# Moving the log-decay sums behind the first chunk's scores in a scan and feed-forward kernel

## The chip, the cores and the metric

The kernel runs on one core of one Trainium2 chip. The metric is the device time of one execution in microseconds (us). Five engines work side by side, each through its own list of instructions in order: TensorE (PE in the rows, its weight loads PEld), VectorE (DVE), ScalarE (ACT), GpSimd (POOL) and SyncE (SP), whose queue issues all DMA transfers here.

## The reference

```python
log_a = np.log(np.clip(a, 1e-06, 1.0))
for c in range(nc):
    cum = np.cumsum(la, axis=-1)                      # la, xc, Bc, Cc: chunk c
    L = np.exp(cum[:, :, :, None] - cum[:, :, None, :]) * causal
    CB = np.einsum('bhin,bhjn->bhij', Cc, Bc)
    y_intra = np.einsum('bhij,bhjd->bhid', CB * L, xc)
    y_inter = np.einsum('bhin,bhnd->bhid', Cc, state) * np.exp(cum)[:, :, :, None]
    y[:, :, sl] = y_intra + y_inter
    decay_from_j = np.exp(cum[:, :, -1:] - cum)
    Bx = np.einsum('bhjn,bhjd->bhjnd', Bc, xc) * decay_from_j[:, :, :, None, None]
    state = decay_full[:, :, None, None] * state + np.sum(Bx, axis=2)
x = y.transpose(0, 2, 1, 3).reshape(B * S, H * D)     # 3072 tokens, 256 wide
h = x @ w_in                                          # to 2048
out = np.maximum(0.01 * h, h) @ w_out                 # back to 256
```

## The kernel before

The program walks the sequence in 16 chunks of 48 positions, with all 32 pairs of batch and head in one chunk. A chunk has a fixed series of steps: `scores` (TensorE, C times B, into a PSUM tile `sc`), a decay exponential `decay_exp` (ScalarE, from a PSUM tile `pd` into `lt`), `weigh` (VectorE, scores times decays), `state_decay` (GpSimd, writes the state rows of `lt` from `erev`), `chunk_products` (TensorE, `lt` times `xs`), a transpose into `stage` and copies of the new state into the next chunk's `xs` (`hand_on`). The next chunk's products need these copies, so the chunks form a serial chain. The feed-forward part runs on 512-token tiles beside the later chunks: `ffn_in` (six matmuls into `hp`), an activation into `gh`, a rest `gl`, and `ffn_out`. Weights come as words `raw`, are decoded (`decode_abs` on ScalarE into `mag`, then VectorE) and split into a high part `wh` (ScalarE) and a low part `wl` (GpSimd).

The order of the instructions on every engine is the order in which the Python code is written. Waits between engines are put in by the framework from the tiles that instructions read and write.

The decays come in two ways. Chunks 0 to 2 take `decay_mask` and `decay_direct`, which multiply by `reach` (made on VectorE from the log decays `la`). Chunks 3 to 15 take `decay_stack`, which reads `dl` and `dr`. Part of these are rows of 16-bit pieces of running sums: `sums` (L222) multiplies `la` by `ends_at` into the PSUM tile `first`, `split_sums` (L228) makes three 16-bit parts in four passes (L232 ScalarE, L233 VectorE, L235 ScalarE, L237 VectorE), `save_sums` (L239) stores them to DRAM in two DMAs, and `load_rows` (L248) loads the rows of one chunk in two DMAs, `dl` (L253) and `dr` (L256). `fill_rest` (L208) fills another part of `dr` on ScalarE. `reverse_near` (L600) writes other columns of the same PSUM tile `first` with four small matmuls, and ScalarE's exponential of them (L610) gives `erev`, from which GpSimd makes the state rows (L321).

`keep_warm` (L117) issues matmuls on a zeroed tile `idle` whose result nobody reads; four of them open the program, two more stand at the second feed-forward step (`BRIDGE`).

Of the kernel before, what the change touches and what calls it, by code (L numbers as in the profile page):

```python
# [19 lines left out]
Q = 48  # L20
# [9 lines left out]
TS = 512  # L30
LAG = 3
OUT_AT = {1: 0, 2: 1, 3: 2, 4: 3, 5: 4, 8: 5}
WARM = 4
BRIDGE = {1: 2}
RAWS = 3
SLOTS = 2
# [25 lines left out]
def scan_ffn(ctx: ExitStack, tc: tile.TileContext, a_l, c_l, d_l, x_l, w_l, out_l):  # L62
# [46 lines left out]
    def fetch_x(c, eng=nc.sync):  # L109
        alloc_x(c)  # L110
        for rows in [slice(h * R + N, h * R + R) for h in range(2)] if c > 1 else [slice(0, 2 * R)]:
            eng.dma_start(xss[c][rows].rearrange("p h b d -> p (h b d)"), x_l[c, rows])
# [1 line left out]
    idle = const.tile([128, 944], BF16, name="idle")  # L114
    nc.vector.memset(idle[:, :128], 0.0)

    def keep_warm(space, n):  # L117
        for _ in range(n):
            nc.tensor.matmul(
                space, lhsT=idle[:, :128],  # L120
                rhs=idle[:, :128].unsqueeze(1).to_broadcast([128, TS // 128, 128]),
                start=True, stop=True,
            )

    nc.scalar.preload_act_table_set("natural_log_exp_and_others")
    first = banks()
    keep_warm(first[:, 1], WARM)

    la = pe.tile([128, NC * NM], F32, name="la")
    nc.sync.dma_start(la, a_l)  # L130
# [77 lines left out]
    def fill_rest(b):  # L208
        nc.scalar.copy(
            dr[:Q, b].rearrange("q m i -> q (m i)").bitcast(F32).rearrange(  # L210
                "q (m i) -> q m i", m=NM
            ),
            later[:Q].bitcast(F32).unsqueeze(1).to_broadcast([Q, NM, Q // 2]),
        )
# [7 lines left out]
    def sums(space):  # L222
        for hf in range(2):
            nc.tensor.matmul(
                space[:, hf, :2 * Q], lhsT=la[:R + Q, hf * 128:(hf + 1) * 128],
                rhs=ends_at[:R + Q].rearrange("p g i -> p (g i)"), start=True, stop=True,
            )

    def split_sums(space):
        total = space[:, :, :2 * Q].rearrange("p f (g i) -> p f g i", i=Q)  # L230
        p = [parts[:, :, :, i] for i in range(3)]
        nc.scalar.copy(p[0], total)  # L232
        nc.vector.tensor_tensor(out=rest, in0=total, in1=p[0], op=ALU.subtract)  # L233
        yield
        nc.scalar.copy(p[1], rest)  # L235
        yield
        nc.vector.tensor_tensor(out=p[2], in0=rest, in1=p[1], op=ALU.subtract)  # L237

    def save_sums(f, eng=nc.sync):  # L239
        eng.dma_start(  # L240
            left_d[:, f * 8:(f + 1) * 8].rearrange("g c m t i -> (c m) g (t i)"),
            parts[:, f].rearrange("p g t i -> p g (t i)"),
        )
        eng.dma_start(
            right_d[f * 8:(f + 1) * 8].rearrange("c m q i -> (c m) (q i)"),
            parts[:, f].rearrange("p g t i -> p (g t i)"),
        )
# [20 lines left out]
    def decay_direct(c, space):  # L268
        for k in range(2):
            for g in range(2):  # L270
                h, rows = half(g, 2 * k), slice(g * R, g * R + Q)
                nc.tensor.matmul(
                    space[h * R:(h + 1) * R, k, :8 * Q], lhsT=after[rows, g],
                    rhs=reach[c][rows, 8 * k:8 * k + 8], start=False, stop=True,
                )
# [29 lines left out]

    spread = {}

    def spread_c(c):
        if c >= SPREAD:
            spread[c] = ins[c][:, C_AT:].rearrange("p (b e i) -> p b e i", b=NB, e=2)  # L310
            return
        cs = spread[c] = pcs.tile([128, NB, 2, Q], F32, name="cs")
        src = ins[c][:, C_AT:NEAR].rearrange("p (b i) -> p b i", b=NB)
        for e in range(2):
            nc.scalar.activation(cs[:, :, e], src, AF.Copy, scale=mine[:, e:e + 1])

    def state_decay(c):
        if c + 1 == NC:
            return
        alloc_lt(c)  # L320
        nc.gpsimd.tensor_tensor(  # L321
            out=lts[c].rearrange("q p b e r -> q (p b e) r")[:, :, :N],
            in0=ins[c][:, N_AT:N_AT + NM * N].rearrange("p (m n) -> p m n", n=N),
            in1=erev[:, c * NM:(c + 1) * NM].unsqueeze(2).to_broadcast([128, NM, N]),
            op=ALU.mult,
        )
# [187 lines left out]
    def ffn_in(s, warm=0):  # L514
        t, f = steps[s]
        assert f in ready
        hp = hps[s] = ps_h.tile([128, TS], F32, name="hp")
        keep_warm(hp, warm)
        n = 0
        for h, x in ((0, xh), (0, xl), (1, xh)):  # L520
            for k in range(2):
                nc.tensor.matmul(  # L522
                    hp, lhsT=w_half[h][:, f, k * 128:(k + 1) * 128], rhs=x[t][:, k, :],
                    start=(n == 0), stop=(n == 5),
                )
                n += 1
        ghs[s] = pg.tile([128, TS], F32R, name="gh")
        gls[s] = pg.tile([128, TS], F32R, name="gl")
        nc.scalar.activation(ghs[s], hp, AF.Prelu, alpha=0.01)  # L529
# [45 lines left out]
    with tc.tile_pool(name="ps_d", bufs=2, space=PSUM, reuse_waits="tile") as ps_d:  # L575

        def free_tile():
            return ps_d.tile([128, 2, TS], F32, name="pd")
# [23 lines left out]
        def reverse_near(space, at):  # L602
            for k in range(2):
                for g in range(2):
                    h, rows = half(g, 2 * k), slice(g * R, g * R + Q)
                    nc.tensor.matmul(
                        space[h * R:(h + 1) * R, k, at:at + near // 2], lhsT=after[rows, g],
                        rhs=by_pair(la[:, :near], rows, k), start=True, stop=True,
                    )
            nc.scalar.activation(  # L610
                erev[:, :near].rearrange("q (c k m) -> q k c m", k=2, m=4),
                space[:, :, at:at + near // 2].rearrange("q k (c m) -> q k c m", m=4), AF.Exp,
            )
# [18 lines left out]
            decay_mask(pd)  # L632
        fill_reach(0, 0)
        fill_reach(0, 1)
        sums(first)
        decay_direct(0, pds[0])
        nc.vector.tensor_reduce(out=mine, in_=own, axis=mybir.AxisListType.X, op=ALU.add)
        fill_reach(2, 0)
        splitting = split_sums(first)
        next(splitting)  # L640
        spread_c(0)
        fill_reach(1, 0)
        next(splitting)
        for _ in splitting:
            pass
        fill_reach(1, 1)
        save_sums(0)
        sc = banks()
        scores(0, sc)
        decay_exp(0, pds[0])  # L650
        reverse_near(first, 2 * Q)
        decay_direct(1, pds[1])
        state_decay(0)
        weigh(0, sc)
        spread_c(1)
        decay_exp(1, pds[1])
        fill_rest(3 % SLOTS)
        state_decay(1)
        os = free_tile()
        chunk_products(0, os)  # L660
        fetch_x(2)
        fetch_w(1)
        load_rows(3)
        load_rows(4)
        fetch_c(3)
        scs = {1: banks()}
        scores(1, scs[1])
# [8 lines left out]
        lows(0, os)  # L676
        spread_c(2)
        decay_exp(2, pd)
        fill_rest(4 % SLOTS)
        state_decay(2)  # L680
        decode_shift(0)
        decode_sign(0)
# [5 lines left out]
        for h in range(2):  # L688
            reverse(pd[:, h], rest_of[h], 8 * Q)
        fetch_w(2)  # L690
        fetch_c(4)
        fetch_x(3)
        states(1, os, (1, 2, 0, 2, 1, 2, 0, 0))
# [9 lines left out]
        settle()  # L703
        highs(2, os)
        decode_abs(1)
        lows(2, os)
        turn(2, os)
        decode_shift(1)
# [385 lines left out]
```

## Time and profile before

| | |
|---|---|
| median of 3 runs | 303.44 us (303.3 to 304.85) |
| the profiled execution's own time | 303.38 us |
| its span, first to last instruction | 301.5 us |
| around the span | 1.88 us |
| TensorE busy | 293.6 us (97% of the span) |
| VectorE, ScalarE, GpSimd busy | 218.3, 182.4, 71.9 us |

The profile page is of one execution. Busy shares are averages over stages with different limits; the stages are told apart in the rows further down.

### The profile page before, as it was taken

What the parts mean: (1) busy time and instruction counts of PE and PEld (TensorE: products, weight loads), DVE (VectorE), ACT (ScalarE), POOL (GpSimd) and SP (SyncE); (2) the same over time, 40 slices, a digit from 0 to 9 for tenths busy, and PEclk for the clock granted to TensorE, in tenths of its full rate; (3) what the DMA queues carried; (4) which work ended last, traced back from release to release, by engine and by line L of the source; (5) the groups of instructions that cost most, each with busy time, mean ns of one, the idle gap of its engine ahead of it and who ended that gap; (6) DMA issues with size and microseconds to landing.
All of it is one profiled execution on the core that took longest, in us unless ns stands there. A gap on an engine that the chain in (4) does not pass through costs nothing.

```text
span 301.5 us, 6819 instructions
## 1 busy us (share of the span) xinstructions
PE 293.6 (97%) x2718; PEld 230.9 (77%) x2718; DVE 218.3 (72%) x379; ACT 182.4 (61%) x351; POOL 71.9 (24%) x148
## 2 busy tenths in 40 slices
PE   8889999999999999999999999999999999999995
PEld 4547676777777778888888888888888888888883
DVE  6879979987875688866877887677576565656562
ACT  6989758666755565735555666574665364536452
POOL 7567666866865440000000000000000000000000
PEclk9999999999999999999999999999999999999999
DMA  6697658665532101000100000000030000000004
GB/s 235 213 315 245 199 173 252 206 222 174 161 93 93 28 5 67 0 2 0 70 2 1 0 0 3 0 0 0 2 139 0 0 2 1 0 0 2 0 0 139
DMA packets 12492, 22.95 MB, mean 76 GB/s; under 512 B 4590, under 2 KB 5486, under 8 KB 12462
## 3 DMA queue, kind: packets, MB, share of 16 engines
q1 hardware_dynamic: 12462, 22.53, 23.2%
q8 instruction: 21, 0.34, 0.5%
q14 instruction: 9, 0.07, 0.1%
HBM read 19.08 MB, written 3.44 MB: 75 GB/s over the span
## 4 chain that ended last, share of the span: by engine, by line
PE 89%; DVE 5%; ACT 2%; issue 1%; DMA 1%; POOL 0%; SPq 0%; DVEq 0%
PE sc L776 18%; PE op L806 14%; PE sc L806 14%; PE op L546 14%; PE hp L522 13%; PE hp L776 7%; PE sc L366 3%; PE sc L336 2%; PE sc L280 1%; DVE mag L463 1%; DVE top L468 1%; DMA dr<-right_d 1%; DVE w L477 1%; DVE gl L535 1%; DVE lt L350 1%
## 5 line engine op out<-in xcount | busy, mean ns | idle before, releaser
L412 POOL COPY xs<-stage 16x128 f32<-16x128 f32 x98 | 35.8, 365 | 24.5 <-DVE stage L396 18.2
L529 ACT ACTIVATE gh<-hp 128x512 fp32r<-128x512 f32 x32 | 19.1, 598 | 26.0 <-PE hp L522 25.8
L817 ACT ACTIVATE gh<-u 128x512 fp32r<-128x512 f32 x32 | 20.0, 625 | 17.7 <-DVE u L858 17.7
L546 PE MATMUL op<-gh,wh 128*128 128x512 f32 x64 | 27.9, 436 | 0.0
L821 DVE TENSOR_TENSOR gl<-u,gh 128x512 fp32r<-128x512 f32 x32 | 22.0, 687 | 7.9 <-ACT u L818 7.9
L857 DVE TENSOR_TENSOR u<-sc,kept 128x512 f32<-128x512 f32 x16 | 11.1, 691 | 22.2 <-PE sc L776 22.2
L817 ACT ACTIVATE gh<-kept 128x512 fp32r<-128x512 f32 x16 | 10.1, 633 | 28.1 <-DVE kept L866 28.1
L817 ACT ACTIVATE gh<-hp 128x512 fp32r<-128x512 f32 x16 | 9.6, 598 | 26.8 <-PE hp L776 26.8
L546 PE MATMUL op<-gl,wh 128*128 128x512 f32 x64 | 25.2, 394 | 0.4 <-DVE gl L535 0.4
L866 DVE TENSOR_TENSOR kept<-sc,kept 128x512 f32<-128x512 f32 x16 | 11.1, 692 | 19.4 <-PE sc L776 19.3
L546 PE MATMUL op<-gh,wl 128*128 128x512 f32 x64 | 25.0, 390 | 0.0
L806 PE MATMUL op<-gl,wh 128*128 128x512 f32 x64 | 24.9, 389 | 0.0
L806 PE MATMUL sc<-gl,wh 128*128 128x512 f32 x64 | 24.9, 389 | 0.0
L806 PE MATMUL sc<-gh,wl 128*128 128x512 f32 x64 | 24.9, 389 | 0.0
L806 PE MATMUL op<-gh,wh 128*128 128x512 f32 x64 | 24.9, 389 | 0.0
L806 PE MATMUL op<-gh,wl 128*128 128x512 f32 x64 | 24.9, 389 | 0.0
L806 PE MATMUL sc<-gh,wh 128*128 128x512 f32 x64 | 24.9, 389 | 0.0
L350 DVE TENSOR_TENSOR lt<-sc,lt 128x384 f32<-128x384 f32 x32 | 16.3, 550 | 10.7 <-ACT gh L529 8.1
L535 DVE TENSOR_TENSOR gl<-hp,gh 128x512 fp32r<-128x512 f32 x32 | 21.7, 677 | 3.1 <-ACT hp L532 3.1
L491 POOL TENSOR_TENSOR wl<-w,wh 128x512 fp32r<-128x512 f32 x16 | 20.7, 1301 | 9.6 <-ACT wh L490 9.4
L522 PE MATMUL hp<-xh,wh 128*128 128x512 f32 x64 | 20.3, 398 | 0.8 <-ACT xh L423 0.6
L818 ACT ACTIVATE u<-u 128x512 f32<-128x512 f32 x32 | 20.2, 632 | 1.0
(147 smaller groups left out, 733.1 us busy)
## 6 DMA issues: line engine op xcount, KB each, us to landing
raw<-w_l SPq DMA_DIRECT2D x16, 512.0 KB, 4.1
bcn<-d_l SPq DMA_DIRECT2D x13, 448.0 KB, 5.1
xs<-x_l SPq DMA_DIRECT2D x28, 96.0 KB, 3.4
out_l<-ob SPq DMA_DIRECT2D x10, 256.0 KB, 2.0
bcn<-c_l SPq DMA_DIRECT2D x3, 352.0 KB
xs<-x_l SPq DMA_DIRECT2D x2, 256.0 KB, 5.1
out_l<-ob SPq DMA_DIRECT2D x4, 128.0 KB
dl<-left_d SPq DMA_DIRECT2D x13, 9.0 KB, 3.7
```

The source lines that it names most:

```text
L350: nc.vector.tensor_tensor(out=to, in0=at, in1=to, op=ALU.mult)
L412: copy(xss[c + 1][h * R:h * R + N, 2 * p:2 * p + 2, bs], stage[rows, :, bs],)
L491: nc.gpsimd.tensor_tensor(out=wl[:, f], in0=w32s[f], in1=wh[:, f], op=ALU.subtract)
L522: nc.tensor.matmul(hp, lhsT=w_half[h][:, f, k * 128:(k + 1) * 128], rhs=x[t][:, k, :], start=(n == 0), stop=(n == 5),)
L529: nc.scalar.activation(ghs[s], hp, AF.Prelu, alpha=0.01)
L535: nc.vector.tensor_tensor(out=gls[s], in0=hps.pop(s), in1=ghs[s], op=ALU.subtract)
L546: nc.tensor.matmul(op, lhsT=w_half[h][:, f, DM + m * 128:DM + (m + 1) * 128], rhs=x, start=(start and i == 0), stop=(last and i == 2),)
L776: nc.tensor.matmul(bank, lhsT=w[h], rhs=x[g], start=start and i == 0, stop=i == 2, skip_group_check=True,)
L806: nc.tensor.matmul(outs[t][m], lhsT=w_half[h][:, f, DM + m * 128:DM + (m + 1) * 128], rhs=x, start=start and i == 0, stop=last and i == 2,)
L817: nc.scalar.activation(gh, h, AF.Prelu, alpha=0.01)
L818: nc.scalar.activation(in_place, h, AF.Prelu, alpha=0.01)
L821: nc.vector.tensor_tensor(out=gl, in0=g, in1=gh, op=ALU.subtract)
```

## The change

- The two `sums` matmuls leave their place ahead of the first `decay_direct`; two dummy matmuls of 512 and 384 columns (`BETWEEN`) stand there. The sums now come behind `reverse_near`.
- `split_sums` moves behind `weigh(0)`, its passes between the two halves of `spread_c(1)`; its last pass goes from VectorE to GpSimd.
- `save_sums(0)` comes behind `fetch_x(2)`, and `load_rows(3)` and `load_rows(4)` move behind `fetch_w(2)`.
- `fill_rest` for chunk 3 takes the place of that for chunk 4, which moves behind `decode_abs(1)`.

```diff
+BETWEEN = (4, 3)
-    def keep_warm(space, n):
-        for _ in range(n):
+    def keep_warm(space, lengths):
+        for n in lengths:
             nc.tensor.matmul(
-                space, lhsT=idle[:, :128],
-                rhs=idle[:, :128].unsqueeze(1).to_broadcast([128, TS // 128, 128]),
+                space[:, :n * 128], lhsT=idle[:, :128],
+                rhs=idle[:, :128].unsqueeze(1).to_broadcast([128, n, 128]),
                 start=True, stop=True,
             )
...
-        nc.vector.tensor_tensor(out=p[2], in0=rest, in1=p[1], op=ALU.subtract)
+        nc.gpsimd.tensor_tensor(out=p[2], in0=rest, in1=p[1], op=ALU.subtract)
...
-        sums(first)
+        keep_warm(first[:, 1], BETWEEN)
         decay_direct(0, pds[0])
         nc.vector.tensor_reduce(out=mine, in_=own, axis=mybir.AxisListType.X, op=ALU.add)
         fill_reach(2, 0)
-        splitting = split_sums(first)
-        next(splitting)
         spread_c(0)
         fill_reach(1, 0)
-        next(splitting)
-        for _ in splitting:
-            pass
         fill_reach(1, 1)
-        save_sums(0)
         sc = banks()
         scores(0, sc)
         decay_exp(0, pds[0])
         reverse_near(first, 2 * Q)
+        sums(first)
         decay_direct(1, pds[1])
         state_decay(0)
         weigh(0, sc)
-        spread_c(1)
+        spread_c(1, (0,))
+        splitting = split_sums(first)
+        next(splitting)
+        spread_c(1, (1,))
+        next(splitting)
         decay_exp(1, pds[1])
-        fill_rest(3 % SLOTS)
         state_decay(1)
+        for _ in splitting:
+            pass
         os = free_tile()
         chunk_products(0, os)
         fetch_x(2)
+        save_sums(0)
         fetch_w(1)
-        load_rows(3)
-        load_rows(4)
         fetch_c(3)
...
-        fill_rest(4 % SLOTS)
+        fill_rest(3 % SLOTS)
...
         fetch_w(2)
+        load_rows(3)
+        load_rows(4)
         fetch_c(4)
...
         decode_abs(1)
+        fill_rest(4 % SLOTS)
         lows(2, os)
```

TensorE's list from the first decay matmuls to the first chunk's products, before (in brackets the semaphores that a row waits for; the words `DVE`, `Activation`, `Pool` and `DMAHW` in their names say whose work it is):

```order
L224 MATMUL sc<-ends_at,la 128x96 [waits DMAHW0_49,Activation_49,Pool_49]
...
L272 MATMUL pd<-reach_134,after 64x384 [waits DVE_49,Pool_49]
...
L336 MATMUL sc<-cs,bcn 64x96 [waits DMAHW1_49,Activation_49]
...
L606 MATMUL sc<-la,after 64x24 [waits DVE_49]
...
L272 MATMUL pd<-reach_135,after 64x384 [waits DVE_49]
...
L366 MATMUL pd<-lt,xs 32x64 [waits DMAHW2_49,DVE_49,Pool_49]
```

The sums (L224) are the first of these, and the rows left out repeat the ones shown. The same stretch of the changed kernel, its lines numbered by the new file:

```order
L120 MATMUL sc<-idle 128x512
...
L120 MATMUL sc<-idle 128x384
L273 MATMUL pd<-reach_134,after 64x384 [waits DVE_49,Pool_49]
...
L339 MATMUL sc<-cs,bcn 64x96 [waits DMAHW1_49,Activation_49]
...
L609 MATMUL sc<-la,after 64x24 [waits DMAHW0_49]
...
L225 MATMUL sc<-ends_at,la 128x96 [waits Activation_49]
...
L273 MATMUL pd<-reach_135,after 64x384 [waits DVE_49]
...
L369 MATMUL pd<-lt,xs 32x64 [waits DMAHW2_49,DVE_49,Pool_49]
```

The dummies wait for nothing; the sums stand between the small matmuls of `reverse_near` and the second `decay_direct`, and now wait for ScalarE alone. (Tile `sc` is also the name under which `first` is printed, since `banks` makes both.)

ScalarE's list over the same stretch, before:

```order
L232 CAST parts<-sc 128x4x48 [waits PE_49]
L315 ACTIVATE cs<-bcn,mine 128x4x48 [waits DMAHW1_49,DVE_49]
...
L235 CAST parts<-rest 128x4x48 [waits DVE_49]
L299 ACTIVATE lt<-pd 128x2x4x48 [waits PE_49]
...
L610 ACTIVATE erev<-sc 128x2x6x4 [waits PE_49]
L315 ACTIVATE cs<-bcn,mine 128x4x48 [waits DMAHW3_49]
...
L209 COPY dr<-later 48x384 [waits Activation_49]
L412 COPY xs<-stage 16x2x64 [waits DMAHW4_49,DVE_49]
```

One cast stands ahead of the first pair `cs`, one behind it, and the copy into `dr` ahead of the state copies. The changed kernel:

```order
L318 ACTIVATE cs<-bcn,mine 128x4x48 [waits DMAHW1_49,DVE_49]
...
L300 ACTIVATE lt<-pd 128x2x4x48 [waits PE_49]
...
L613 ACTIVATE erev<-sc 128x2x6x4 [waits PE_49]
L318 ACTIVATE cs<-bcn,mine 128x4x48 [waits DMAHW3_49]
L233 CAST parts<-sc 128x4x48 [waits PE_49]
L318 ACTIVATE cs<-bcn,mine 128x4x48
L236 CAST parts<-rest 128x4x48 [waits DVE_49]
...
L415 COPY xs<-stage 16x2x64 [waits DMAHW4_49,DVE_49]
```

The two casts of the sums moved to between and behind the second pair `cs`, and the copy into `dr` is gone from here. (Between the last two rows stand the two exponentials of chunk 1, as before.)

SyncE's list of DMAs from the first stores to the fourth chunk's input, before:

```order
L240 DMA left_d<-parts 128x2x144 [waits DVE_49]
L244 DMA right_d<-parts 128x288 [waits DMAHW0_49]
L112 DMA xs<-x_l 48x512 [waits DMAHW2_49,DMAHW1_49,PE_49]
...
L94 DMA raw<-w_l 128x2048 [waits DMAHW3_49]
L253 DMA dl<-left_d 48x2x48 [waits DMAHW7_49,DMAHW4_49]
L256 DMA dr<-right_d 6x16x48 [waits DMAHW5_49,DMAHW0_49]
...
L103 DMA bcn<-d_l 128x896 [waits Pool_49]
```

The stores come first, and one large transfer (`raw`) stands between them and the row loads. The changed kernel:

```order
L113 DMA xs<-x_l 48x512 [waits DMAHW2_49,PE_49]
...
L241 DMA left_d<-parts 128x2x144 [waits DMAHW1_49,Pool_49]
L245 DMA right_d<-parts 128x288
L95 DMA raw<-w_l 128x2048 [waits DMAHW3_49]
L104 DMA bcn<-d_l 128x896 [waits DMAHW4_49]
L95 DMA raw<-w_l 128x2048 [waits DMAHW5_49]
L254 DMA dl<-left_d 48x2x48 [waits DMAHW6_49,DMAHW1_49]
L257 DMA dr<-right_d 6x16x48 [waits DMAHW7_49,DMAHW2_49]
```

The stores went behind the load of chunk 2's `xs`, and between them and the first row loads there are now three large transfers where one stood. The row loads wait for their stores as before (`DMAHW1` and `DMAHW2` are the stores' semaphores here).

## Rows read from the trace of the kernel before

**Rows 1.** Stretches: us; busy of PE, PEld, DVE, ACT, POOL; clock, DMA share, GB/s.

```profile
0.00:24.00 24.00, 20.55 (x460) 11.80 (x464) 18.84 (x51) 19.69 (x51) 14.51 (x35) 1.00 0.79 255
...
60.00:140.00 80.00, 80.00 (x1019) 62.61 (x1007) 60.14 (x108) 48.23 (x94) 31.54 (x69) 1.00 0.26 80
```

**Rows 2.** Chain that ended last, 7 to 10 us: start us, us, what.

```profile
7.15 0.29 PE sc L606 x8
...
7.46 0.22 ACT erev L610
...
7.75 0.63 POOL lt L321
...
8.43 0.87 PE pd L366 x53
...
9.33 0.46 DVE stage L396
```

**Rows 3.** TensorE's timeline, 2.7 to 8 us: start us, us, instruction, count.

```profile
2.73 1.49 PE L262 MATMUL pd<-later,bars 112*128 112x384 bf16 x4
4.01 1.04 PE L224 MATMUL sc<-ends_at,la 112*128 112x96 f32 x4
4.99 1.35 PE L272 MATMUL pd<-reach,after 48*64 48x384 f32 x8
6.26 0.89 PE L336 MATMUL sc<-cs,bcn 32*64 32x96 f32 x32
...
7.22 0.91 PE L272 MATMUL pd<-reach,after 48*64 48x384 f32 x8
```

**Rows 4.** TensorE's timeline, 13 to 14 us.

```profile
13.38 0.71 PE L616 MATMUL pd<-la,after 112*128 112x80 f32 x4
```

**Rows 5.** ScalarE's timeline, 5 to 10 us; brackets: idle before it and releaser.

```profile
5.31 0.80 ACT L315 ACTIVATE cs<-bcn,mine 128x192 f32<-128x192 f32 x2
6.01 0.34 ACT L235 CAST parts<-rest 128x192 bf16<-128x192 f32 x1
...
8.26 0.86 ACT L299 ACTIVATE lt<-pd 128x384 f32<-128x384 f32 x2
9.00 0.51 ACT L209 COPY dr<-later 48x384 f32<-48x384 f32 x1
9.81 0.94 ACT L412 COPY xs<-stage 16x128 f32<-16x128 f32 x3 [0.30 <-DVE stage L396]
```

**Rows 6.** VectorE's timeline, the sums' second pass.

```profile
5.45 0.36 DVE L233 TENSOR_TENSOR rest<-sc,parts 128x192 f32<-128x192 f32 x1 [0.18 <-ACT parts L232]
```

**Rows 7.** GpSimd's timeline, 7 to 11 us.

```profile
7.75 1.52 POOL L321 TENSOR_TENSOR lt<-bcn,erev 128x256 f32<-128x256 f32 x2 [0.89 <-ACT erev L610]
9.90 0.94 POOL L412 COPY xs<-stage 16x128 f32<-16x128 f32 x3 [0.62 <-POOL lt L321]
```

**Rows 8.** ScalarE's timeline, 16 to 19 us.

```profile
17.63 1.22 ACT L412 COPY xs<-stage 16x128 f32<-16x128 f32 x4 [0.53 <-DVE stage L396]
```

**Rows 9.** SyncE's queue, 6 to 12 us: start us, us of issuing.

```profile
6.77 0.39 SPq L240 DMA_DIRECT2D left_d<-parts  x1
...
9.32 1.47 SPq L112 DMA_DIRECT2D xs<-x_l  x2
```

**Rows 10.** Time from issue to landing of the row loads (tile dl), then of tile xs.

```profile
DMA to landing us min/median/max: 2.6/3.7/4.2
DMA to landing us min/median/max: 2.1/3.8/5.1
```

**Rows 11.** TensorE's timeline, 18 to 22 us.

```profile
18.15 0.50 PE L280 MATMUL sc<-dr,dl 102*128 102x384 bf16 x2
...
20.17 0.73 PE L522 MATMUL hp<-xh,wh 128*128 128x512 f32 x2 [0.16 <-ACT wh L490]
...
21.62 0.73 PE L522 MATMUL hp<-xh,wl 128*128 128x512 f32 x2 [0.25 <-DMA dr<-right_d]
```

**Rows 12.** GpSimd's timeline, 20 to 22 us.

```profile
20.26 1.30 POOL L491 TENSOR_TENSOR wl<-w,wh 128x512 fp32r<-128x512 f32 x1 [0.48 <-ACT wh L490]
```

More of the change, by code (lines that the diff above doesn't have):

```diff
@@ L126, in scan_ffn @@
     first = banks()
-    keep_warm(first[:, 1], WARM)
+    keep_warm(first[:, 1], (TS // 128,) * WARM)
     la = pe.tile([128, NC * NM], F32, name="la")
@@ L306, in scan_ffn, with spread_c @@
     spread = {}
-    def spread_c(c):
+    def spread_c(c, es=(0, 1)):
         if c >= SPREAD:
@@ L311, in spread_c @@
             return
-        cs = spread[c] = pcs.tile([128, NB, 2, Q], F32, name="cs")
+        if c not in spread:
+            spread[c] = pcs.tile([128, NB, 2, Q], F32, name="cs")
+        cs = spread[c]
         src = ins[c][:, C_AT:NEAR].rearrange("p (b i) -> p b i", b=NB)
-        for e in range(2):
+        for e in es:
             nc.scalar.activation(cs[:, :, e], src, AF.Copy, scale=mine[:, e:e + 1])
@@ L517, in ffn_in @@
         hp = hps[s] = ps_h.tile([128, TS], F32, name="hp")
-        keep_warm(hp, warm)
+        keep_warm(hp, (TS // 128,) * warm)
         n = 0
```

## The prediction

> **What bounds the kernel now.** I read the stretches of the span first, since the change touches only the opening. From 60 to 140 us TensorE is busy all the time; in the first 24 us it is busy for 20.55 [rows 1]. The reader is to see that all of the change lies in those 24 us: the matmuls behind them are the same in both kernels, so what counts is how much earlier or later the opening hands over.
>
> In the opening I read the chain that ended last. From 7.15 us it goes through the four small matmuls of `reverse_near`, ScalarE's `erev`, GpSimd's state rows, chunk 0's products at 8.43 and the transpose at 9.33 [rows 2]. Then chunk 1 needs the copies of the state, chunk 2 needs chunk 1's, and the first feed-forward tile needs chunk 2's outputs. So the start of chunk 0's products, 8.43, is the number to follow: nothing I find behind it on that chain gives time back.
>
> **The change part by part.**
>
> *Dummies for sums.* The last four matmuls before the place have 384 columns each and start 0.32 us apart (2.73 to 4.01, a quarter of it) [rows 3]. That is 1.2 columns a ns, the lower of the clock's two levels, although the clock column says 1.00 [rows 1]. The dummies have 512 + 384 columns: 0.43 + 0.32 = 0.75 us, so `decay_direct(0)` can start at 4.01 + 0.75 = 4.76 instead of 4.99, 0.23 earlier. It does not gain all of that. The first `decay_direct` took 4.99 to 6.26 = 1.27, the second 0.91 less the 0.08 by which a group's row overlaps the next one (4.99 + 1.35 against 6.26), so 0.83 [rows 3]: the clock rose inside the first. If it rises at the same moment, the piece that is done earlier is done at half speed, and of 0.23 some 0.11 stays. Scores then start at 6.26 - 0.11 = 6.15. Bounds: nothing, and 0.5 (0.23 + 1.27 - 0.83 is 0.67, but then `cs` is late: it takes 0.80 and before started at 5.31 [rows 5]). I take 0.11, since the work on TensorE before this place is unchanged.
>
> *The sums at their new place.* The list shows that they wait for ScalarE. Not for the logarithms of `la`: the scores ahead of them already waited for `cs`, which ScalarE makes after those. What is left is `erev`, which reads other columns of the same PSUM tile `first`; the kernel before has the mirror of this, where `reverse_near` waited for VectorE, which had read the sums' columns. So TensorE, which runs in order, stops behind `reverse_near` until ScalarE has read. `erev` ran from 7.46 to 7.68 [rows 2]; 0.11 earlier and with a hand-over of 0.05 (7.68 to 7.75 includes one) the sums start at about 7.62. Their price there: the two nearest matmuls, of the same form with 80 and 128 columns, took 0.71 less 0.08 = 0.63 [rows 4]; at the old place, at the lower clock for the most part, the sums took 4.01 to 4.99 = 0.98 [rows 3]. I take 0.63, as the clock is up by then. Behind them is queued `decay_direct(1)`, 0.83. So chunk 0's products start at 7.62 + 0.63 + 0.83 = 9.08, where GpSimd's rows would have let them start at 8.43 - 0.11. Against 8.43 that is **+0.65 us**. With the sums at 0.98 it is +1.0; with the whole 0.5 gained ahead it is +0.26.
>
> *Casts on ScalarE, subtractions on VectorE and GpSimd.* Two casts (0.34 each [rows 5]) and VectorE's pass (0.36 [rows 6]) leave the stretch ahead of chunk 0's scores; neither was what the products waited for. At the new place they must be done before the state copies. Sums done 8.25 + 0.08; cast to 8.7; VectorE's pass to 9.1 (second half of `cs` meanwhile); second cast to 9.5; exponentials of chunk 1, 0.86 [rows 5], to 10.36. The copies are due at 9.81 + 0.65 = 10.46, so the cover is 0.1 us thin: any further delay is paid one for one. GpSimd's subtraction starts at 9.55 and costs between 0.36 (VectorE's) and 0.76 (one of the two larger ones in 1.52 [rows 7]); it ends by 10.3, and its copies are due at 9.90 + 0.65 = 10.55. It stands inside GpSimd's old idle time of 0.62 [rows 7]. Zero for all of these.
>
> *The fills of `dr`.* The first, 0.51 at 9.00, stood ahead of an idle time of 0.30 [rows 5]; taking it away only makes room for the casts. The other now stands before the state copies at 17.63, behind an idle time of 0.53 [rows 8]: it fits with 0.02 to spare. Zero, bound 0.1.
>
> *Stores and row loads.* The stores were issued at 6.77 and now stand behind the pair for `xs`, issued from 9.32 for 1.47 [rows 9]: 9.32 + 0.65 + 1.47 = 11.44 and, after 0.39, 11.83. SyncE stops at the row loads until the stores have landed; behind it are queued chunk 4's input, chunk 3's `xs` and a weight, none needed for several us. A store's landing is not shown; the row loads' 2.6 to 4.2 [rows 10] is the nearest row, and I use it for both. Then `dr` lands between 11.83 + 2.6 + 2.6 = 17.0 and 11.83 + 4.2 + 4.2 = 20.2. `decay_stack(3)` needs it at 18.15 + 0.65 = 18.80, and TensorE has idle times of 0.16 and 0.25 soon behind it [rows 11], so 19.2 is free. (The second is put down to a DMA, but GpSimd's `wl` ended at 20.26 + 1.30 = 21.56 [rows 12], which is what that matmul reads.) I take the near half, since when the stores go out the large transfers are still behind them: zero, up to 1.0.
>
> **Sum.** The profiled execution took 303.38 us, 301.5 of span and 1.88 around it, 0.06 under the median of the runs. 303.38 + 0.65 = 304.03: **304.0 us**, 0.2% slower, which one can't tell from no change. A difference under 0.5% (1.5 us) is about what a measurement of this kernel can't tell.
>
> **The rivals.**
>
> *The early scores carry through.* If the sums don't stop for `erev`, or the clock rises earlier behind the dense dummies, TensorE reaches the products at 7.22 - 0.11 + 0.63 + 0.83 = 8.57 (+0.14, 303.5), or with 0.5 gained ahead at 8.18 (-0.25, 303.1). For it speaks that the columns don't overlap; against it, that the list has the wait.
>
> *Row loads late: clearly slower.* One mechanism, at `decay_stack(3)`: the loads sit behind a weight, an input and another weight. If both store and load take the longest landing of an `xs` row, 5.1 [rows 10], `dr` lands at 11.83 + 10.2 = 22.0, 2.8 past what is free: 306.8. It decides from a landing at 20.1 on, where 304.03 + 0.9 passes 304.96. For it: the two medians of 3.7 together already give 19.2. Against: the stores go out into a queue of small transfers. The Trainium skill (DMA: Bandwidth & Descriptors, Latency and other measured facts) says that the access to HBM takes 0.2 us on average but 2 us at high load and is the main part of a transfer's fixed cost. By that rule the loads, which run beside the large transfers, come near the long end, 305.0, and the stores near the short one; no run so far shows the two apart.
>
> *The thin cover breaks.* If the hand-overs between TensorE, ScalarE, VectorE and ScalarE again cost 0.18, as the idle time ahead of VectorE's pass does [rows 6], instead of the 0.05 that I put in, four of them make 0.5, of which 0.1 is covered: 304.4.
>
> **How the numbers follow.** The stop behind `erev` with little else: 0.55 (303.7 to 304.3). Early scores carried through: 0.17 (303.0 to 303.6). Thin cover: 0.14 (304.2 to 304.8). Row loads past 20.1: 0.09 (305.0 to 306.8). Something not seen: 0.05, both ways. The range 303.1 to 304.9 leaves out the late loads and half of the unseen. Faster by over 0.5% (under 301.9): no case reaches it, 0.02. Slower by over 0.5%: the late loads and a little of the unseen, 0.10. Within: 0.88.
>
> **What would show it.** Right: scores start near 6.15; an idle time of 0.3 to 0.5 us on TensorE ahead of the sums, released by `erev`; products at about 9.1 with `decay_direct(1)` directly ahead; transpose near 10.0; the shift of 0.65 still there at the first feed-forward matmul and at 60 us. `decay_stack(3)` shows no wait for a DMA. Wrong: the sums right behind `reverse_near`, products at or before 8.43; an idle time ahead of `decay_stack(3)` released by `dl` or `dr`; state copies that wait for ScalarE's or GpSimd's own earlier work; or a shift that shrinks on the way to 37 us because another wait had been the later one.

## The result and the profile after

The changed kernel takes 305.84 us (median of 22 runs, 303.98 to 308.58), the kernel before 303.31 (22 runs, 302.94 to 304.87) in the same comparison: a ratio of 1.0074, 95% interval 1.0050 to 1.0097. It is slower by 0.5 to 1.0%, where 0.2% and a range of 303.1 to 304.9 were predicted. (The quotient of the two medians is 1.0083. Six of the 22 runs of the kernel before lie at 304.7 to 304.9, over 1 us above the rest, and a median does not see them.)

The profiled execution took 304.22 us, a span of 302.1 and 2.12 around it, which looks like the 304.03 of the sum. It is one of the short ones, and it gets there in another way. Its TensorE timeline in the opening, against [rows 3] and the products of [rows 2] (start us, us, instruction, count, idle time before it and its releaser):

```profile
4.01 0.95 PE L120 MATMUL sc<-idle 128*128 128x512 bf16 x2
4.90 1.03 PE L273 MATMUL pd<-reach,after 48*64 48x384 f32 x8
5.86 0.89 PE L339 MATMUL sc<-cs,bcn 32*64 32x96 f32 x32
6.68 0.31 PE L609 MATMUL sc<-la,after 48*64 48x24 f32 x8
7.32 0.69 PE L225 MATMUL sc<-ends_at,la 112*128 112x96 f32 x4 [0.33 <-ACT erev L613]
7.93 0.88 PE L273 MATMUL pd<-reach,after 48*64 48x384 f32 x8
8.74 0.86 PE L369 MATMUL pd<-lt,xs 64*32 64x64 f32 x64
```

The stop behind `erev` is there, 0.33. From the scores to the products it is 8.74 - 5.86 = 2.88 us, where 9.08 - 6.15 = 2.93 was forecast and 2.17 stood before. But the scores start at 5.86 and not at 6.15, so the opening loses 0.31 and not 0.65. This 0.31 is still there at the first feed-forward matmul, 16.74 where the kernel before has 16.42.

The same view from 16 us on, against [rows 11], and the piece of the chain that ended last which ends at the second row:

```profile
16.74 0.73 PE L525 MATMUL hp<-xh,wh 128*128 128x512 f32 x2 [0.60 <-ACT xh L426]
...
19.93 0.50 PE L281 MATMUL sc<-dr,dl 102*128 102x384 bf16 x2 [1.29 <-DMA dl<-left_d]
...
21.43 0.81 PE L525 MATMUL hp<-xh,wh 128*128 128x512 f32 x2
```

```profile
15.22 4.67 DMA dl<-left_d
```

`decay_stack(3)` starts 1.78 later than before (19.93 against 18.15), and 1.29 of that is a wait for chunk 3's row load `dl`. That is the sign that the prediction named for the rival "Row loads late". In this execution the next idle times take part of it back: the second feed-forward tile is 1.26 later (21.43 against 20.17), and further down the span the matmuls are 0.6 later, as is the span.

SyncE's queue, against [rows 9], shows how the load came to be late:

```profile
9.63 1.43 SPq L113 DMA_DIRECT2D xs<-x_l  x2
11.15 0.40 SPq L241 DMA_DIRECT2D left_d<-parts  x1
11.59 0.47 SPq L245 DMA_DIRECT2D right_d<-parts  x1
12.10 0.43 SPq L95 DMA_DIRECT2D raw<-w_l  x1
12.58 0.45 SPq L104 DMA_DIRECT2D bcn<-d_l  x1
13.07 2.05 SPq L95 DMA_DIRECT2D raw<-w_l  x1
15.22 0.38 SPq L254 DMA_DIRECT2D dl<-left_d  x1
```

Stores at 11.15 and 11.59 (forecast 11.44 and 11.83); then a weight, an input and a second weight, whose issue alone took 2.05; the load at 15.22, and 4.67 to its release. SyncE waits for no store here: the load goes out 0.1 us after the weight's issue has ended (13.07 + 2.05 = 15.12). Before, no DMA wait stood at this place.

The times of the 22 runs lie far apart, and this can't be understood without the granted clock of each: in 8 of them its mean is 0.994 and the time 306.79 to 308.58; in the 14 others it is 0.998 to 1.0 and the time 303.98 to 306.74. The median of those 14 is 304.95, still 1.6 above the kernel before, so the clock is the smaller part of the loss. The kernel before has no run below 0.998 in the 97 that stand beside the experiments. What an execution loses around its span is 2.16 us in the mean of the 22, and 1.91 in the 22 runs of the kernel before in the next comparison: 0.25 more. Some 0.1 of it comes with both moves in SyncE's list (2.01 in the queue experiment below, 1.89 and 1.88 with one move alone); the cause no run here shows.

### The profile page after: what moved, and what is told of

Its sections match the earlier page's. It is cut to its first block, busy times and chain, and to the rows that moved or that the text cites. A ratio compares the mean times of both kernels' runs of the same rounds, so it can differ in the third digit from the quotient of the medians.

```text
span 302.1 us, 6822 instructions
## 1 busy us (share of the span) xinstructions
PE 293.3 (97%) x2720; PEld 230.9 (76%) x2720; DVE 217.1 (72%) x378; ACT 182.8 (61%) x351; POOL 72.3 (24%) x149
## 4 chain that ended last, share of the span: by engine, by line
PE 88%; DMA 5%; SPq 2%; POOL 1%; issue 1%; ACT 1%; DVE 1%; DVEq 0%
PE sc L781 18%; PE op L811 14%; PE sc L811 14%; PE op L549 14%; PE hp L525 11%; PE hp L781 7%; PE sc L369 3%; DMA raw<-w_l 2%; PE sc L339 2%; DMA dl<-left_d 2%; PE sc L281 1%; DMA xs<-x_l 1%; POOL xs L415 1%; SPq L95 1%; PE sc L120 1%
## 5 line engine op out<-in xcount | busy, mean ns | idle before, releaser
L871 DVE TENSOR_TENSOR kept<-sc,kept 128x512 f32<-128x512 f32 x16 | 11.1, 691 | 19.5 <-PE sc L781 19.3
```

## The experiments

Theory A: the row loads of chunk 3 land after TensorE wants them, because stores and loads both went back in SyncE's queue, and the wait costs twice, once itself and once by the clock behind it. Rivals: the opening (B: the stop and the dummies) carries the loss, or an execution's clock does, whatever the order. (The C of the first expectation is another one: the whole DMA queue runs late.)

**The row loads ahead of the second weight.** The changed kernel with

```diff
-        fetch_w(2)
         load_rows(3)
         load_rows(4)
+        fetch_w(2)
```

> The changed kernel with the four row loads ahead of the second weight (fetch_w(2)) instead of behind it; all else as changed. Theory A (the row loads of chunk 3 come late behind that weight; TensorE stops at decay_stack(3), and in many executions the granted clock then falls to a mean of 0.994): dr lands about 2 us sooner, near 17.5 us, no DMA wait ahead of decay_stack(3) or one under 0.4 us, granted clock 1.000 in nearly all executions, median 303.3 to 304.0. Theory B (the sums' stop behind erev and the longer TensorE list ahead of the first products set the time): within 0.5 us of the changed kernel's median, 305.3 to 306.3, with the same spread. Theory C (the DMA queue as a whole runs late, so weights become the later wait): about half, 304.3 to 305.2, with waits for raw still there.

Measured: 304.58 (12 runs, 303.49 to 305.05) against 303.32 (22 runs), ratio 1.0021, interval 0.9999 to 1.0043; no run below clock 0.998. Its SyncE queue and TensorE:

```profile
12.96 0.38 SPq L254 DMA_DIRECT2D dl<-left_d  x1
...
14.55 0.36 SPq L95 DMA_DIRECT2D raw<-w_l  x1
```

```profile
18.73 0.50 PE L281 MATMUL sc<-dr,dl 102*128 102x384 bf16 x2 [0.31 <-DMA dl<-left_d]
```

Most of the loss is gone with the whole opening left as it is, and the wait is 0.31. For A, against B as the main cost. The median misses the 303.3 to 304.0 of A and lies in the range of C, but in this profile (303.58) ScalarE's decoding waits for no weight. The load is not fast here either: it is there 5.7 us after its issue, but the issue comes 2.3 earlier.

**The moves in SyncE's queue alone**, in the kernel before:

```diff
-        save_sums(0)
...
         fetch_x(2)
+        save_sums(0)
         fetch_w(1)
-        load_rows(3)
-        load_rows(4)
         fetch_c(3)
...
         fetch_w(2)
+        load_rows(3)
+        load_rows(4)
```

> The kernel before with nothing changed but SyncE's list: the stores behind the load of chunk 2's xs, the row loads behind the second weight. Sums, casts, fills and dummies stay where they were. Theory A: the whole loss comes with the list alone: a wait of 1 us or more for dl or dr ahead of decay_stack(3), executions with a granted clock of 0.994, median 304.8 to 306.5. Theory B: nothing but the list has moved, so 303.2 to 303.6, as before.

Measured: 306.24 (11 runs, 303.37 to 308.05), ratio 1.0075, interval 1.0049 to 1.0102: all of the change's loss without its opening. The profiled execution (306.82, mean clock 0.994), its load's piece of the chain, its TensorE, and its stretches (us; busy of PE, PEld, DVE, ACT, POOL; clock, DMA share, GB/s):

```profile
13.62 7.28 DMA dl<-left_d
```

```profile
20.94 0.50 PE L280 MATMUL sc<-dr,dl 102*128 102x384 bf16 x2 [2.72 <-DMA dl<-left_d]
...
22.34 1.03 PE L119 MATMUL hp<-idle 128*128 128x512 bf16 x2
22.81 1.42 PE L522 MATMUL hp<-xh,wh 128*128 128x512 f32 x2
```

```profile
21.00:22.00 1.00, 1.00 (x30) 0.68 (x34) 0.00 (x0) 0.53 (x2) 1.00 (x2) 0.99 0.17 60
22.00:23.00 1.00, 1.00 (x17) 0.51 (x7) 0.47 (x1) 1.00 (x3) 0.61 (x2) 0.50 0.76 287
...
24.00:25.00 1.00, 1.00 (x4) 0.78 (x3) 0.97 (x2) 0.00 (x0) 0.00 (x0) 0.50 1.03 200
```

Both prices show. The wait, 2.72. Then, a little more than a microsecond after it, a granted clock of 0.50, the 1.2 GHz level: the two dummies take 1.03 and the pair behind them 1.42, where [rows 11] has 0.73 for the pair and the kernel before has for the dummies

```profile
19.41 0.60 PE L119 MATMUL hp<-idle 128*128 128x512 bf16 x2
```

The shift against the kernel before is -0.09 us at 16 us, 2.64 at the second feed-forward tile and 3.4 from 26 us on.

**The row loads later still**, in the changed kernel, and the changed kernel once more beside it:

```diff
-        load_rows(3)
-        load_rows(4)
         fetch_c(4)
         fetch_x(3)
+        load_rows(3)
+        load_rows(4)
```

> The changed kernel with the row loads one place further back, behind chunk 4's input and chunk 3's xs: the suspected cost is made larger. Theory A: dr lands 1.5 to 3 us later than in the changed kernel, the wait ahead of decay_stack(3) grows to 2.5 to 5 us, the granted clock falls in nearly every execution, median 307 to 310 with less spread of the clock. Theory B: as the changed kernel, 305.3 to 306.3.

> The changed kernel once more, for a second profile and further pairs of time and granted clock. Theory A: executions with a mean clock under 0.996 are over 306 us and those at 1.000 are mostly under 305.2; a profiled execution of the slow kind shows a longer wait ahead of decay_stack(3) than the 1.29 us of the first profile, and matmuls at half rate behind it. Theory B: time and clock have no relation.

Measured: 309.05 (4 runs, 308.03 to 310.16), ratio 1.0187, interval 1.0150 to 1.0225, clock 0.989 or 0.994 in all four; the changed kernel again 306.44 (4 runs), 1.0113, interval 1.0073 to 1.0154. TensorE with the later loads, and then in the repeated changed kernel (305.5, clock 1.00):

```profile
22.05 0.82 PE L281 MATMUL sc<-dr,dl 102*128 102x384 bf16 x2 [3.92 <-DMA dl<-left_d]
22.80 1.56 PE L339 MATMUL sc<-bcn 32*64 32x96 f32 x32
```

```profile
4.90 1.56 PE L273 MATMUL pd<-reach,after 48*64 48x384 f32 x8
6.39 0.95 PE L339 MATMUL sc<-cs,bcn 32*64 32x96 f32 x32
...
9.33 0.86 PE L369 MATMUL pd<-lt,xs 64*32 64x64 f32 x64
...
20.75 0.50 PE L281 MATMUL sc<-dr,dl 102*128 102x384 bf16 x2 [1.52 <-DMA dl<-left_d]
```

The wait grows with the lateness of the loads, and the time with it. The repeat shows how much one opening varies: the first `decay_direct` keeps the lower clock to its end here (1.56 where the profile after has 1.03), and the products start at 9.33 instead of 8.74. Its profile is the one of its four runs whose clock did not fall; the other three (0.994 or less) take 306.29 to 308.88.

**TensorE kept busy through the wait.** The changed kernel with ten dummies of 512 columns ahead of `decay_stack(3)`:

```diff
             space = banks()
+            if s == 0:
+                keep_warm(space[:, 0], (TS // 128,) * 10)
             decay_stack(LEAD + s, space)
```

> The changed kernel with ten dummy matmuls of 512 columns (2.15 us at the full rate) ahead of decay_stack(3), where TensorE otherwise waits for the row loads: the wait stays as long, but TensorE works through it. Theory A in its second half (the fall of the granted clock after the wait costs 1 to 2 us by itself): no execution under 0.998, none over 306.5, median 304.7 to 305.4. If only the wait costs: median and spread as the changed kernel, 305.3 to 306.3 and up to 308, or higher by what the dummies take where the loads come early.

Measured: 305.67 (12 runs, 305.07 to 305.95), ratio 1.0044, interval 1.0024 to 1.0064; no run below clock 0.998.

```profile
19.22 2.33 PE L120 MATMUL sc<-idle 128*128 128x512 bf16 x10
21.44 0.50 PE L281 MATMUL sc<-dr,dl 102*128 102x384 bf16 x2
```

The dummies cost a fixed 2.2 us there, and the second price is gone: the runs spread over 0.9 us instead of the 4.6 of the changed kernel. So at this place the clock falls because TensorE stands idle, and not in some executions whatever the order. The median lies in the other half of the expectation (305.3 to 306.3, only the wait costs), since every execution pays the 2.2 us of the dummies; that the clock has a price of its own is told by the clock and the spread.

**The kernel before with stores later, the loads kept ahead of the second weight** (they stand behind `fetch_c(3)` and not directly behind the first weight):

```diff
-        save_sums(0)
...
         fetch_x(2)
+        save_sums(0)
         fetch_w(1)
-        load_rows(3)
-        load_rows(4)
         fetch_c(3)
...
+        load_rows(3)
+        load_rows(4)
         fetch_w(2)
```

> The kernel before with the stores behind chunk 2's xs and the row loads behind chunk 3's input, ahead of the second weight: the list of the loads-ahead experiment with the old sums. It tells whether the 1.26 us that this experiment still lost come from the list or from the sums' place. From the list: 304.0 to 304.6. From the sums (stop and longer TensorE list): 303.2 to 303.6.

Measured: 304.02 (12 runs, 302.62 to 305.50) against 303.48 (35 runs), ratio 0.9990, interval 0.9966 to 1.0015: no difference. (The median is 0.5 higher, but 15 of the 35 runs of the kernel before lie at 304.7 and above; the means are 304.01 and 304.08.) Where the loss that the loads-ahead experiment still had comes from stays open: the median says the list, the ratio says not the list, and the intervals of the two experiments overlap. The profile has the loads issued at 12.88 and no wait for them, but its mean clock is 0.994 all the same: the first feed-forward pair, at 16.63, takes 1.22 instead of 0.73, so `decay_stack(3)` came to them only at 19.10. The clock can fall in this stretch without a late row load, then; one run of the twelve shows it (and two of twelve with the stores alone moved, below), where 6 of 11 did in the queue experiment.

**Each move alone**, in the kernel before: only the loads behind the second weight, then only the stores behind chunk 2's input.

> The kernel before with nothing changed but the place of the row loads, which stand behind the second weight as in the changed kernel; the stores stay early. If a row load lands late because of the large transfers queued ahead of it, the loads are issued near 12.5 us, 1.1 earlier than with the stores moved too (13.62), but stand behind the same three transfers: decay_stack(3) still waits for dl, for 1.0 to 2.5 us, and the median is 304.6 to 306.3. If they were late because SyncE and the loads have to wait for late stores, the stores issued at 6.8 us are long landed here: no wait at decay_stack(3), 303.2 to 303.8.

> The kernel before with nothing changed but the place of the stores, which stand behind chunk 2's input as in the changed kernel; the row loads stay behind the first weight. If the large transfers ahead of the loads make them late, only one weight stands ahead of them here: dl lands before 18.2 us, no wait at decay_stack(3) or one under 0.4, median 303.2 to 304.2. If late stores make the loads late, it waits for 1.0 us and more, 304.6 to 306.

Measured: loads alone 303.58 (12 runs) against 303.54, ratio 0.9990, interval 0.9967 to 1.0014. Stores alone 304.47 (12 runs), 1.0026, interval 0.9997 to 1.0056. Both expectations missed in one half: three large transfers ahead of the loads cost nothing measurable by themselves, and stores at 10.09 us make no wait at `decay_stack(3)`. Where the loads are issued in the two profiles, and what TensorE does; loads alone first:

```profile
13.59 0.38 SPq L253 DMA_DIRECT2D dl<-left_d  x1
```

```profile
4.96 1.56 PE L272 MATMUL pd<-reach,after 48*64 48x384 f32 x8
6.45 1.56 PE L336 MATMUL sc<-cs,bcn 32*64 32x96 f32 x32
...
8.17 1.54 PE L272 MATMUL pd<-reach,after 48*64 48x384 f32 x8
9.63 1.18 PE L366 MATMUL pd<-lt,xs 64*32 64x64 f32 x64
...
20.15 0.50 PE L280 MATMUL sc<-dr,dl 102*128 102x384 bf16 x2
```

```profile
12.84 0.33 SPq L253 DMA_DIRECT2D dl<-left_d  x1
```

```profile
18.33 0.50 PE L280 MATMUL sc<-dr,dl 102*128 102x384 bf16 x2
...
23.46 0.75 PE L366 MATMUL sc<-lt,xs 64*32 64x64 f32 x38 [0.60 <-DMA xs<-x_l]
```

From the load's issue to its use there are 20.15 - 13.59 = 6.6 us and 18.33 - 12.84 = 5.5 (the first of these executions runs 1.99 late at this place, so its 6.6 may be more than most have). In the kernel before it was 18.15 - 11.35 = 6.8. With both moves the use without the wait would be at 18.22 in the queue experiment, 4.6 after the issue at 13.62; in the profile after, 18.64 - 15.22 = 3.4. The loss needs both moves, and these figures, each from one profile, say why: each move takes only part of that time. (With the stores alone the lateness turns up elsewhere: chunk 3's `xs` holds TensorE for 0.60.)

**Chunk 3's row loads in another queue.** The changed kernel with these two issued by ScalarE, at its place behind the first fill of `dr`, and not by SyncE (`load_rows` takes the issuing engine as a second argument there):

```diff
         fetch_w(2)
-        load_rows(3)
+        load_rows(3, nc.scalar)
         load_rows(4)
```

> The changed kernel, with chunk 3's two row loads issued by ScalarE into its own queue instead of SyncE's, where ScalarE has made the first fill of dr, near 14.0 us; ScalarE's copies of xs behind them move by the two issues, some 0.8 us. If a row load lands late because it stands in one queue behind a weight, an input and a second weight, it lands here as with little ahead of it, 2.6 to 4.2 us after the issue, by 18.2 at the latest: decay_stack(3) does not wait for dl, and what is left is ScalarE's 0.8, so 304.5 to 305.5. If it lands late because the DMA engines are busy with whatever queue, it still takes 4.7 to 7.3: a wait of 0.5 to 2 us there, 305.5 to 307.

**The row loads ahead of the first weight**, in the changed kernel:

```diff
         save_sums(0)
+        load_rows(3)
+        load_rows(4)
         fetch_w(1)
...
         fetch_w(2)
-        load_rows(3)
-        load_rows(4)
```

> The changed kernel, with both chunks' row loads directly behind the stores, ahead of the first weight. SyncE stops at them until the stores have landed, so the loads go out near 13 us with no large transfer ahead of them. If what makes them late is the transfers ahead, they land by 17: no wait for dl at decay_stack(3), and the price is the first weight, issued 2 to 3 us later than 12.1, for which ScalarE's decoding and the casts wait: 304.5 to 306. If it is the time from the issue that counts alone (4.7 to 7.3 whatever stands ahead), they land at 17.7 to 20.3: a wait of 0 to 1.7 at decay_stack(3) beside the weight's, 305 to 307.5.

Measured: other queue 304.33 (12 runs, 303.67 to 306.71), ratio 1.0027, interval 1.0004 to 1.0051; the profiled execution is one of the two with clock 0.994 (306.55). Loads first 305.75 (6 runs, 305.21 to 307.00), ratio 1.0076, interval 1.0047 to 1.0105. The issue and TensorE in the first, then in the second:

```profile
12.82 0.35 ACTq L254 DMA_DIRECT2D dl<-left_d  x1
```

```profile
20.53 0.50 PE L281 MATMUL sc<-dr,dl 102*128 102x384 bf16 x2 [2.10 <-DMA dl<-left_d]
```

```profile
11.75 0.39 SPq L241 DMA_DIRECT2D left_d<-parts  x1
...
13.65 0.33 SPq L254 DMA_DIRECT2D dl<-left_d  x1
```

```profile
18.99 0.50 PE L281 MATMUL sc<-dr,dl 102*128 102x384 bf16 x2
20.69 0.89 PE L339 MATMUL sc<-bcn 32*64 32x96 f32 x32 [1.19 <-DMA bcn<-d_l]
```

In the other queue the load was still not there 7.7 us after its issue in this execution, one of the two longest, so the place in SyncE's queue is not all that makes it slow. Yet ten of the twelve runs lie between 303.67 and 305.14, and the median is below both ranges of the expectation: the earlier issue (12.82, where 14.0 was expected) seems to have helped in most executions, of which there is no profile. With the loads first SyncE waits 0.9 for the store, which takes 11.75 to 13.65 = 1.90 to land. Nothing on TensorE then waits for the loads, and the price is paid by what now stands behind: the input, 1.19, and the weight, for which ScalarE's decoding waits 2.20.

**The opening, two pieces of it**, both on the kernel with the row loads ahead of the second weight. `decay_direct(1)` ahead of the sums, which takes the stop away, and then no dummies:

```diff
         reverse_near(first, 2 * Q)
-        sums(first)
         decay_direct(1, pds[1])
+        sums(first)
```

> The kernel of the loads-ahead experiment (four row loads ahead of the second weight) with one line moved: decay_direct(1) stands ahead of the sums, so that ScalarE has read erev by the time TensorE comes to them. The stop behind erev took 0.33 us there and the distance from the start of the scores to the start of chunk 0's products was 2.88 us (2.17 in the kernel before). Theory B as a smaller second term: no stop, distance 2.4 to 2.6, median 0.3 to 0.5 under 304.58, so 304.1 to 304.3. If the stop costs nothing in the end: 304.4 to 304.8.

```diff
-BETWEEN = (4, 3)
+BETWEEN = ()
```

> The kernel of the loads-ahead experiment without the two dummies between. If the dummies help the clock up: the first decay_direct runs at the lower rate for longer (1.3 us or more from its start to the scores), scores near 6.2, median 0.3 to 1.0 over 304.58, more spread. If not: decay_direct(0) starts when its operand is there, near 4.5, scores between 5.4 and 6.2 as with dummies, median 304.3 to 304.8.

Measured: without the stop 304.64 (12 runs), ratio 1.0007, interval 0.9987 to 1.0028, which is not told apart from the 1.0021 with it. Without the dummies 307.05 (12 runs), 1.0071, interval 1.0035 to 1.0107, in two groups: five runs at 303.69 to 304.71 and seven at 306.88 to 307.85. TensorE without the stop, then without the dummies (307.77):

```profile
6.39 1.13 PE L339 MATMUL sc<-cs,bcn 32*64 32x96 f32 x32
...
7.59 0.85 PE L273 MATMUL pd<-reach,after 48*64 48x384 f32 x8
8.37 0.69 PE L225 MATMUL sc<-ends_at,la 112*128 112x96 f32 x4
8.99 0.86 PE L369 MATMUL pd<-lt,xs 64*32 64x64 f32 x64
```

```profile
4.28 2.01 PE L273 MATMUL pd<-reach,after 48*64 48x384 f32 x8
6.23 1.55 PE L339 MATMUL sc<-cs,bcn 32*64 32x96 f32 x32
...
8.46 1.17 PE L225 MATMUL sc<-ends_at,la 112*128 112x96 f32 x4 [0.33 <-ACT erev L613]
9.56 1.56 PE L273 MATMUL pd<-reach,after 48*64 48x384 f32 x8
```

Taking the stop out shortens scores to products to 2.60, although in this execution the clock rose later. Without the dummies the profiled opening stays at the lower clock beyond 11 us (1.55 for scores that take 0.89 at the higher). So the dummies do help the clock up, and by more than the 0.3 to 1.0 us expected. In this profile the clock falls a second time, to 0.50 from 21 to 24 us, with no wait at `decay_stack(3)` (22.15); five of the twelve runs have a mean clock of 0.994 or less. A late row load is one way to the lower clock, and not the only one.

## Why the prediction was wrong

- **The step that failed: "Stores and row loads", "zero, up to 1.0".** What it had wrong is the landing of chunk 3's row load. It was taken as 2.6 to 4.2 [rows 10]. That row tells of three of the thirteen `dl` loads only: chunk 3's own, 3.7, which stood behind one weight, and two at 38 and 76 us, 4.2 and 2.6. Behind three large transfers the load took 4.67 in the profile after and 7.28 in the queue experiment, where the DMA engines are busy for 0.92 and 0.95 of the time from 13 to 20 us. Of the range that came out of it the near half was taken, on an argument about the stores. And a wait of TensorE was given its length as its price, while the clock that can fall behind it adds to that: 3.4 in all for a wait of 2.72. The bound of 1.0 had neither.
- **The load's time of issue was right by luck.** By the sum it goes out one landing of a store after the stores, at 14.4 to 16.0, and it did, at 15.22. But a store took 1.90 and 2.75 in the two runs in which SyncE does wait for one (loads first; stores alone, 10.09 to 12.84), at or below the short end of 2.6 to 4.2. What held the load back in the profile after was the issue of the transfers ahead, 2.05 for the second weight alone. In the queue experiment this took 0.44, and the load went out at 13.62. The stores went out 0.3 earlier than forecast, as the whole opening did.
- By the rule that the prediction cited from the Trainium skill (DMA: Bandwidth & Descriptors, Latency and other measured facts) such loads come near the long end. The traces agree in direction; 4.67 to 7.7 is beyond the 4.2 at which the prediction ended its range, and how much of it is access to HBM no run here shows. The same page of the Trainium skill (Queues, rings and completion order) says that a DMA engine consumes descriptors of one ring in their order. The landings in the last section agree with this, but the loads in ScalarE's queue took 7.7, so the order within one queue isn't the whole of it.
- The 305.0 that the prediction gives for a store at the short end and a load at the long end does not come out of its rows: 11.83 + 2.6 + 4.2 is 18.6, ahead of the 19.2 that is free, and with 5.1 for the load it is 19.5, or 304.4.
- **The rival "Row loads late: clearly slower"** names what happened: 305.0 to 306.8 at 0.09, measured 305.84. The place and the reason, loads behind a weight, an input and another weight, are as measured. The sum is not: it had 5.1 for the store and 5.1 for the load, where the store took about half of that, the load up to 7.28, and the clock came on top; that the time lies in its range is in part luck. What was said against the rival, that the stores go out into a queue of small transfers, told nothing of the loads, and there the delay sat.
- **The stop behind `erev`** was right in place and size: 0.33 idle, sums 0.61 (forecast 0.63), `decay_direct(1)` 0.81 (0.83), 2.88 to 2.94 in all where 2.93 was forecast.
- **The dummies** took 0.89 to the start of the next matmul and not 0.75, and 0.47 (4.02 to 4.49) in the profile with the loads ahead, where the clock rose inside them. The gain ahead of the scores was forecast as 0.11; it was 0.40 in the profile after, 0.61 with the loads ahead, and -0.13 in the repeat. So the opening, forecast at +0.65, cost 0.31, 0.10 and 0.90 (products at 8.74, 8.53 and 9.33 against 8.43). The bounds of zero to 0.5 for the gain were too close by a little on both sides: when the clock rises changes from execution to execution, and one profile of before does not show that.
- **"The thin cover breaks"** did not come: ScalarE's `xs` copies start at 10.12 behind VectorE's transpose (0.21 idle), with the second cast done at 9.13, and GpSimd's subtraction ends at 9.76 ahead of its copies at 10.21, as far behind the transpose as before.
- **Fills: zero** was right. The second stands at 17.59, the state copies behind it at 17.99, 0.36 later than before with an opening 0.3 later.
- **Chances.** "Slower by over 0.5%" had 0.10. One thin row, a wait that nothing bounded from above, deserved more.

What stays open: why the same three transfers ahead of the load let it land after 4.67 us in one execution and 7.28 in another, and why it took 7.7 in another queue. With the loads alone moved it also lands late, 5.3 us after its issue by the trace's semaphore records (13.59 to 18.91), but ahead of TensorE, which came at 20.15 in that execution. How much of the changed kernel's loss is the opening's, and most of the 0.25 us around the span, are not explained either.

## What to carry to other kernels

When DMA issues are moved back in a queue, follow the last one of them to its use: the issue times of everything it now stands behind, a landing taken from a transfer that had as much queued ahead of it, and the time left until its first reader. Where that is short on TensorE, price the wait above its length, because the clock can fall behind it; a few dummies in the wait, or the small loads ahead of the large ones, keep the loss bounded. And a kernel whose opening lies near a rise of the clock has more than one time, so one profile of it is one sample.

## What the runs showed of the hardware

- A TensorE idle for 2.72 us (released at 20.94) was followed by a granted clock of 0.50 from about 22 us to past 25. Waits of 2.10 (other queue) and 3.92 (later loads) also went with a clock of 0.50, waits of 1.29 and 1.52 in two profiled executions of the changed kernel did not. Of 26 runs of the changed kernel 11 have a mean clock of 0.994 or less; with dummies through the wait, none of 12.
- When the clock rises in the opening differs between executions of the same code. The kernel with the loads alone moved has the opening of before up to 9 us. Its profile (305.38) shows `decay_direct(0)` at 1.56, scores at 1.56 and the second `decay_direct` at 1.54, where [rows 3] have 1.35, 0.89 and 0.91, although the clock column says 1.00. It is 1.99 us behind at the first feed-forward tile and stays so. Its other runs lie at 302.98 to 303.72 (9) and at 304.88 and 305.01; the kernel before has the same two groups on that chip, 14 runs at 302.94 to 303.59 and 9 at 304.87 to 305.48. That these 9 are openings at the lower clock is likely from this, but no profile of the kernel before caught one.
- One DMA issue in the row of transfers behind the stores often takes 1.1 to 2.05 us in SyncE's queue instead of 0.3 to 0.5. It is not always the same one: the second weight in the profile after, a store (1.08) with the loads ahead, a second `dl` (1.11) in the queue experiment.
- A small load lands right behind the large transfer that stands directly ahead of it in its queue. By the semaphore records of the traces, chunk 3's `dl` lands 0.2 to 0.4 us behind that transfer in eleven of the thirteen profiles in which SyncE issues it: 15.02 behind 14.65 in the kernel before, 19.88 behind 19.71 in the profile after, 20.89 behind 20.71 in the queue experiment, 18.69 behind 18.50 with the loads ahead. With nothing large ahead (loads first) it lands 2.6 us after its issue, and with one weight ahead 3.7 us after it (the kernel before, stores alone).
- The last few packets can make such a load late. By the packet records of the queue experiment, 372 of the 384 packets of 96 bytes that the four row loads of chunks 3 and 4 consist of had started by 18.50, and the last 12 started only from 19.86 on. What held them back no run here shows.
